# Operand sums among the last row stages, shorter column steps, stored low parts and two more banks for the chains of a fused GLU and spectral kernel

## The chip, the cores and the metric

The kernel runs on one core of one Trainium2 chip. The metric is device time in microseconds (us) for one execution; where several executions are shown, their median counts. Five engines work side by side and meet at semaphores: TensorE (PE, with its weight loads PEld), VectorE (DVE), ScalarE (ACT), GpSimd (POOL) and SyncE (SP). POOL and SP mainly issue DMAs here, each in the order of its own queue, and each waits in that queue until the data of a transfer is ready.

## The reference

For 2048 tokens of 576 features the reference mixes two branches with a gate per token:

```python
g = sigmoid((x * gate_w).sum(-1, keepdims=True))
a = irfft2(rfft2(x) * (w_r + 1j * w_i), s=(S, D))           # S = 2048, D = 576
b = (gelu(x @ w_gate) * (x @ w_up)) @ w_down                # 576 -> 4608 -> 576
return g * a + (1 - g) * b
```

Everything is float32.

## The kernel before, in words

**The dense branch.** It is all on PE. Each float32 operand is split into a high and a low part of a format that PE takes in one pass, and a product is three matmuls (high by high, low by high, high by low). The 4608 hidden features are 36 tiles of 128, taken in 18 blocks of two; the tokens are two halves of 1024, and each half is two pieces `tb` of 512. `chain` (L717) makes one hidden tile of the gate or the up projection for one piece: 14 matmuls of 512 columns into one PSUM bank `pgu`, of which there are two. `hidden` (L757) calls two chains, then GELU on ACT (L767), the product with the second bank on DVE (L771), a high copy on ACT and a low part on DVE (L775). `down` (L805) multiplies such tiles with the down weights, 24 matmuls of 288 columns for a pair of token tiles, into the two buffers of `pdn`, which ACT scales and moves out (L814); POOL then adds the result in DRAM (`yd`, L802). Weights come by SP into `raws`, ACT copies their high part into `gu` or `dn` (L213), and DVE makes the low part (L708).

**The products.** In the second token half, from block `FIRST` on, `products` (L1001) replaces the eight chains of a block by a scheme of seven block products with 14 matmuls each, which needs the sums and differences of quarters of the input, `s1` to `s4`. `operands` (L882) makes these on DVE and ACT in three pieces, from inputs that `load_xs` (L878) brings into `xraw`.

**The spectral branch.** It runs on DVE and ACT beside the chains, in a generator: `forward_rows` (a transform along the features, L481) for each token half, `first_tiles` (L401, a radix-4 step over the tiles with its twiddle factors), `columns` (L234), `last_tiles` (L414) and `inverse_rows` (L532) for each half. Its results are scaled by the gate and added in DRAM. The column stage goes through 16 blocks, pipelined over 18 steps of `STEP` gaps each. In one step `g` counts gaps: a forward product on PE at `g` 0 (`product`, L269, six matmuls of 290 columns into the tile `pf2` of two banks), its real part copied out at 1, the filter at 2, the weights at 5, the end of the filter at 6; the inverse product of the block before at 4, copied out at 5. Two rows of each block have to change places: `corner` (L249) sends them out to `cns` and back by four small DMAs, the first pair two steps ahead at `g` 0, the second at `g` 3; the high copy that reads the block is at `g` 1 of the next step. A second generator, `beside`, fills what is left with radix-4 steps over the tiles.

**The order.** The order of all work is written out by the Python code. `gap()` (L635) is called twice in every chain and after every `down`; there it takes steps of the generator. Each yielded cost is charged against a credit that PE work earns, so the vector work is spread evenly along PE's. Each engine executes its own list in order. What is late in an engine's list holds back everything behind it.

Of the kernel before, what the change touches and what calls it, by code (L numbers as in the profile page):

```python
# [30 lines left out]
STEP = 7  # L31
FIRST = 5
# [71 lines left out]
def _twiddles(eng, act, unit, real, imag, places, tmps, sgn, cost):  # L104

    todo = list(places)

    def scaled(i):
        if i < len(todo):
            at, n = todo[i]  # L110
            s = 1.0 if n == 4 else sgn * math.sin(math.pi * n / 8)
            act.activation(tmps[i % len(tmps)][0], unit(*at), AF.Copy, scale=s)

    yield None
    for i in range(2):
        scaled(i)
    yield None
    for i, (at, n) in enumerate(todo):
        scaled(i + 2)
# [6 lines left out]
        eng.scalar_tensor_tensor(xr, xr, c, ti, op0=ALU.mult, op1=ALU.subtract)  # L126
        yield cost
        eng.scalar_tensor_tensor(xi, xi, c, tr, op0=ALU.mult, op1=ALU.add)
        yield cost
# [28 lines left out]
def _build(nc, tc, a):  # L158
    with ExitStack() as ctx:
# [3 lines left out]
        spec = ExitStack()  # L163
        psf = spec.enter_context(tc.tile_pool(name="psf", bufs=1, space=bass.MemoryType.PSUM))
# [39 lines left out]
        def ps_f2():  # L204
            return psf.tile([P, 2, 512], F32, name="pf2", tag="pf2", bufs=1)

        ps7 = []

        def ps_one():
            return ps7[0].tile([P, TB], F32, name="pone", tag="pone", bufs=2)  # L210
# [19 lines left out]
        def columns():  # L230
# [38 lines left out]
            def product(d, kb, h, l):  # L269
                v = ps_f2()  # L270
# [22 lines left out]
            def beside():  # L293

                more = gates()
                for d in range(1, 4):
                    yield from four(d, TAKEN, sp, -1)
                    made[0] = d
# [4 lines left out]
                yield from more  # L303

            for s in range(2):
                for kb in range(2):
                    load_cc(s, kb)
            yield from four(0, TAKEN, sp, -1)
# [13 lines left out]
            for kb in range(18):  # L322
# [18 lines left out]
                for g in range(STEP):  # L341
# [29 lines left out]
                    elif g == 5:  # L371
                        if was:
                            copy(two(Z[kb - 1]), w[:, :, :NK])
# [3 lines left out]
                    elif g == 6:  # L377
# [9 lines left out]
            gone[0] = 20 * STEP  # L387
            for c in side.pop():
                yield c
# [11 lines left out]
        def first_tiles(h):  # L401

            sp = tmp[:, 0:2 * SW].rearrange("p (e k) -> p e k", e=2)
            tmps = [tmp[:, SW * i:SW * (i + 1)] for i in range(4)]
            tmps = [(x, x[:, 0:NK], x[:, NK:]) for x in tmps]
# [3 lines left out]
            places = [((k, TAKEN[o]), o * k) for k in range(1, 4) for o in range(1, 4) if TAKEN[o] // 2 == h]  # L409
            yield from _twiddles(vec, act, lambda d, e: T[:, d, e], lambda d, e: T[:, d, e, re],  # L410
                                 lambda d, e: T[:, d, e, im], places, tmps, -1, 0.5)
            yield None

        def last_tiles():  # L414
# [3 lines left out]
            tmps = [rows[:, SW * i:SW * (i + 1)] for i in range(4, 8)]  # L418
            tmps = [(x, x[:, 0:NK], x[:, NK:]) for x in tmps]
            places = [((k, LEFT[o]), o * k) for k in range(1, 4) for o in range(1, 4)]  # L420
            yield from _twiddles(vec, act, lambda d, e: T[:, d, e], lambda d, e: T[:, d, e, re],
                                 lambda d, e: T[:, d, e, im], places, tmps, 1, 0.5)
# [109 lines left out]
        def inverse_rows(h):  # L532
            rows = rows_tile()
            T, R = spread(h, rows)
            pl.memset(rows.rearrange("p (c k) -> p c k", c=2)[:, :, 8 * KF:], 0.0)
            yield from moved(lambda t, c: (R[:, c, t, 0:KF], T[:, t, c, 0:KF]))
# [5 lines left out]
            if h == 1:  # L542
                load_xs(0)
# [18 lines left out]
            ))  # L562
            R = rows.rearrange("p (k t) -> p t k", t=8)
            yield None
            if h == 1:
                c = cns.rearrange("p q k -> p (q k)")
                spare_rows = (c[:, 0:D], c[:, D:2 * D], misc[:, SW:SW + D])
                todo_t = list(range(8))
                work = operands()
                n = 0  # L570
                while todo_t or not ops.get("done"):
                    if n % 5 == 0 and todo_t:
                        t = min(todo_t, key=lambda t: abs(count[0] - added[8 + t] - 11))
                        o = spare_rows[len(todo_t) % 3]
                        todo_t.remove(t)
                        act.activation(o, R[:, t, 0:D], AF.Copy, scale=gs[:, 8 + t:9 + t])
                        at(2, lambda t=t, o=o: pl.dma_start(yd[8 + t], o, accum_op=ALU.add))
                    n += 1
# [41 lines left out]
        side = []  # L620
        credit = [0.0]
# [83 lines left out]

        def lower(key, g, r, cost):
            def run():
                vec.tensor_tensor(g[:, 1], r, f(g[:, 0]), ALU.subtract)  # L708
                credit[0] -= cost

# [11 lines left out]

        def chain(j, s, tb):
            due(("gu", j))
            ps, w = ps_gu(), gu[j % 3]
# [13 lines left out]
        def first_chains():  # L739

            v = ps_f2()
            ps = [v[:, c] for c in range(2)]
# [139 lines left out]
        def operands():  # L882

            sx = pool.tile([P, 16 * SW], F32R, name="sx", tag="til")
            s4 = pool.tile([P, 2 * UNIT], F32R, name="s4", tag="tmp")
            parts = [sx[:, 2048 * i:2048 * (i + 1)].rearrange("p (l t k) -> p l t k", l=2, t=2) for i in range(3)]
            parts.append(s4[:, 0:2048].rearrange("p (l t k) -> p l t k", l=2, t=2))
            tails = [sx[:, 6144 + TB * i:6144 + TB * (i + 1)] for i in range(6)] + [s4[:, 2048:2560]]
            for i in range(4):
                ops["s1 s2 s3 s4".split()[i]] = (parts[i][:, 0], parts[i][:, 1], tails[i])  # L890
            ops["a11"] = (xhi[0][:, 0:2], xlo[0][:, 0:2], tails[4])
            ops["a12"] = (xhi[0][:, 2:4], xlo[0][:, 2:4], tails[5])
            ops["a22"] = (xhi[1][:, 2:4], xlo[1][:, 2:4], tails[6])
            m = misc[:, 0:TB]
            for i in range(3):
                if i:
                    load_xs(i)
                    for _ in range(6):
                        yield None
                a11, a12, a21, a22 = (xraw[:, q] for q in range(4))  # L900
                if i == 2:
                    yield from tails_of([(ops[n][2], x) for n, x in (("a11", a11), ("a12", a12), ("a22", a22))])
                for o, x, z, op in ((m, a21, a22, ALU.add), (a21, a11, a21, ALU.subtract),
                                    (a11, m, a11, ALU.subtract), (a12, a12, a11, ALU.subtract)):
                    vec.tensor_tensor(o, x, z, op)
                    yield 0.72
                sums = (("s1", m), ("s2", a11), ("s3", a21), ("s4", a12))
# [3 lines left out]
                else:  # L911
# [4 lines left out]
                    for n, x in sums:  # L916
                        vec.tensor_tensor(ops[n][1][:, i], x, f(ops[n][0][:, i]), ALU.subtract)
                        yield 0.72
            ops["done"] = True
# [183 lines left out]
        for s in range(2):  # L1103
            copy(g1[:, 0, :, s], w1[:, :, s])
            vec.tensor_tensor(g1[:, 1, :, s], w1[:, :, s], f(g1[:, 0, :, s]), ALU.subtract)  # L1105
        aux += [lambda: None] * 2
# [4 lines left out]
        aux += [lambda: None] * 6  # L1111
        one, fin = gate_part(0, rows0)
        for t in range(8):
            aux.append(lambda t=t: one(t))
        aux.append(lambda: [fin(), gens.append(spectral(rows0))])
        for u in range(8):
            aux.append(lambda u=u: release(u))
# [8 lines left out]
        def reload_x(tb):  # L1126
            for k in range(KT):
                i = KT * tb + k
                aux.append(lambda i=i, k=k: [prep_x(tb, k, xraw[:, i % 4]), load_x(i + 4)])

# [55 lines left out]

        for _, _, key in prev[3]:
            due(key)
        spec.close()
        ps7.append(ctx.enter_context(tc.tile_pool(name="ps7", bufs=1, space=bass.MemoryType.PSUM)))  # L1190
# [66 lines left out]
```

## Time and profile before

| | |
|---|---|
| Median of three executions | 1381.41 us (1381.4, 1381.41, 1383.15) |
| The profiled execution's own time | 1383.23 us |
| Its span, first to last instruction | 1381.5 us |
| ScalarE (ACT) busy | 698.4 us, 51% |
| GpSimd (POOL) busy | 266.6 us, 19% |
| Read from and written to HBM | 110.69 MB, 92.01 MB |

The span is 1.7 us shorter than the profiled execution's own time; the rest lies around the instructions. A busy time is the sum of an engine's records. The records of PE overlap, because matmuls are pipelined, so the pace of PE is read from the starts of its matmuls in the timeline and not from their durations. The list of waits gives, for each pair of lines, the total, the number and the longest of the waits that one ended for the other.

### The profile page before, as it was taken

The numbers are of one execution on the slowest core, as the hardware profiler recorded it, in microseconds if no ns is written. First come the engines' busy times: TensorE is split into PE (matmuls) and PEld (weight loads), VectorE is DVE, ScalarE is ACT, GpSimd is POOL, SyncE is SP. The second block draws the span as 40 slices with busy tenths as digits, with TensorE's granted clock in tenths as the row PEclk, the third lists the DMA queues.
The fourth block names the chain that finished last, engine by engine and source line by source line (L and its number), as shares of the span: only waits on it lengthen the run. The fifth ranks groups of instructions, "written<-read, shape, count | busy, mean of one in ns | idle before, by whom it ended". The sixth has DMA issues, their size and how long they took to land.

```text
span 1381.5 us, 20055 instructions
## 1 busy us (share of the span) xinstructions
PE 1368.6 (99%) x7504; PEld 1208.8 (88%) x7504; DVE 1118.0 (81%) x1635; ACT 698.4 (51%) x1072; POOL 266.6 (19%) x326
## 2 busy tenths in 40 slices
PE   8999999999999999999999999999999999999998
PEld 7888888888898888888888888888888888888887
DVE  6989998989868767499898999567777777777776
ACT  5543454344565565444456343865555555555552
POOL 0022111222222221212123011421112222221111
PEclk9999999999999999999999999999999999999999
DMA  8366766668999998655776665966666666666676
GB/s 304 117 116 117 175 116 105 117 114 190 218 238 246 247 217 203 126 109 94 150 151 131 177 125 92 232 135 131 125 131 131 131 128 131 129 129 127 130 154 172
DMA packets 97329, 211.17 MB, mean 153 GB/s; under 512 B 11856, under 2 KB 22096, under 8 KB 96848
## 3 DMA queue, kind: packets, MB, share of 16 engines
q0 software_dynamic: 45248, 92.56, 44.1%
q1 hardware_dynamic: 51984, 117.34, 27.4%
q8 instruction: 59, 0.97, 0.3%
q14 instruction: 38, 0.31, 0.1%
HBM read 110.69 MB, written 92.01 MB: 147 GB/s over the span
## 4 chain that ended last, share of the span: by engine, by line
PE 96%; ACT 2%; DMA 1%; issue 0%; DVE 0%; SPq 0%; DVEq 0%; ACTq 0%
PE pdn L789 33%; PE pgu L728 12%; PE pgu L730 12%; PE pgu L729 12%; PE pgu L971 3%; PE pgu L973 3%; PE pgu L972 3%; PE pgu L734 3%; PE pgu L735 3%; PE pone L971 3%; PE pone L973 3%; PE pone L972 3%; PE pf L274 2%; PE pgu L974 2%; PE pone L974 1%
## 5 line engine op out<-in xcount | busy, mean ns | idle before, releaser
L802 POOL DMA_DIRECT2D yd<-stg x264 | 229.8, 871 | 1024.5 <-ACT stg L814 995.8
L814 ACT ACTIVATE stg<-pdn,omg 128x576 f32<-128x576 f32 x272 | 201.9, 743 | 410.0 <-PE pdn L789 319.8
L789 PEld LDWEIGHTS pdn<-dn,hb 128*128 128x128 f32 x2808 | 388.7, 188 | 12.5 <-ACT stg L814 1.0
L789 PE MATMUL pdn<-dn,hb 128*128 128x288 f32 x2808 | 397.0, 295 | 1.0 <-ACT stg L814 0.8
L728 PE MATMUL pgu<-xhi,gu 128*128 128x512 f32 x728 | 285.6, 392 | 3.7 <-ACT gl L767 3.7
L729 PE MATMUL pgu<-xhi,gu 128*128 128x512 f32 x728 | 284.4, 391 | 0.4 <-DVE gu L1105 0.4
L730 PE MATMUL pgu<-xlo,gu 128*128 128x512 f32 x728 | 284.6, 391 | 0.0
L728 PEld LDWEIGHTS pgu<-xhi,gu 128*128 128x128 f32 x728 | 137.1, 188 | 30.6 <-ACT gl L767 5.5
L730 PEld LDWEIGHTS pgu<-xlo,gu 128*128 128x128 f32 x728 | 137.0, 188 | 29.9
L729 PEld LDWEIGHTS pgu<-xhi,gu 128*128 128x128 f32 x728 | 137.0, 188 | 25.3 <-DVE gu L1105 0.7
L767 ACT ACTIVATE gl<-pgu 128x512 f32<-128x512 f32 x91 | 54.5, 598 | 135.6 <-PE pgu L735 131.4
L213 ACT ACTIVATE gu<-raws 128x1280 fp32r<-128x1280 f32 (+3 forms) x86 | 88.8, 1033 | 40.0 <-PE pgu L734 31.1
L771 DVE TENSOR_TENSOR gl<-gl,pgu 128x512 f32<-128x512 f32 x91 | 62.2, 683 | 39.9 <-PE pgu L735 38.4
L775 DVE TENSOR_TENSOR hb<-gl,hb 128x512 fp32r<-128x512 f32 x92 | 63.2, 687 | 37.5 <-ACT hb L213 37.5
L789 PEld LDWEIGHTS pdn<-dn,gu 128*128 128x128 f32 x624 | 85.6, 188 | 1.9
L789 PE MATMUL pdn<-dn,gu 128*128 128x288 f32 x624 | 86.8, 295 | 0.0
L734 PE MATMUL pgu<-xtl,gu 128*128 128x512 f32 x182 | 70.8, 389 | 0.0
L735 PE MATMUL pgu<-xtl,gu 128*128 128x512 f32 x182 | 70.8, 389 | 0.0
L708 DVE TENSOR_TENSOR gu<-raws,gu 128x1280 fp32r<-128x1280 f32 x44 | 65.3, 1484 | 1.3 <-ACT gu L213 1.3
L989 DVE TENSOR_TENSOR xraw<-xraw 128x512 f32<-128x512 f32 x52 | 36.0, 693 | 28.8 <-ACT xraw L997 28.3
L213 ACT ACTIVATE hb<-gl 128x512 fp32r<-128x512 f32 x92 | 57.3, 623 | 0.0
L1006 DVE TENSOR_TENSOR gl<-gl,pgu 128x512 f32<-128x512 f32 x52 | 35.6, 684 | 25.7 <-PE pgu L974 25.7
(214 smaller groups left out, 2211.9 us busy)
## 6 DMA issues: line engine op xcount, KB each, us to landing
yd<-stg POOLq DMA_DIRECT2D x264, 288.0 KB, 5.0
raws<-wgu SPq DMA_DIRECT2D x44, 640.0 KB, 4.7
raws<-wd SPq DMA_DIRECT2D x72, 288.0 KB, 2.9
colm<-col POOLq DMA_DIRECT2D x32, 256.0 KB, 6.0
raws<-ws SPq DMA_DIRECT2D x21, 384.0 KB, 5.2
quads<-ws SPq DMA_DIRECT2D x20, 384.0 KB, 4.4
tmp<-wf SPq DMA_DIRECT2D x16, 290.0 KB, 5.8
cns<-til SPq DMA_DIRECT2D x64, 72.5 KB, 4.9
```

The lines of the kernel that those rows point to most:

```text
L213: act.activation(o, i, AF.Copy)
L728: pe.matmul(ps, w[:, 0, k, c], xhi[tb][:, k], start=k == 0, stop=False)
L729: pe.matmul(ps, w[:, 1, k, c], xhi[tb][:, k], start=False, stop=False)
L730: pe.matmul(ps, w[:, 0, k, c], xlo[tb][:, k], start=False, stop=False)
L734: pe.matmul(ps, w[:, 0, 4, c], xtl[tb], start=False, stop=False)
L735: pe.matmul(ps, w[:, 1, 4, c], xtl[tb], start=False, stop=True)
L789: pe.matmul(ps[half], h[:, l, c], d[:, q, half * HD:(half + 1) * HD], start=part == 0 and n == 0, stop=part == 1 and n == 2)
L802: pl.dma_start(yd[u], o, accum_op=ALU.add)
L814: put(u, lambda o: act.activation(o.rearrange("p (c k) -> p c k", c=2), v[:, :, 0:HD], AF.Copy, scale=omg[:, u:u + 1]), i == 0)
L971: pe.matmul(ps, hi[:, c], xh[:, t], start=t == 0, stop=False)
L972: pe.matmul(ps, lo[:, c], xh[:, t], start=False, stop=False)
L973: pe.matmul(ps, hi[:, c], xl[:, t], start=False, stop=False)
```

## The change

- **`FIRST` goes from 5 to 4.** One block more of the second token half is made by `products`, so the operands must be ready one block sooner.
- **Operand sums among row stages.** `operands` runs from `woven` inside the last `inverse_rows`: after every second step of the row stages it may take one step, at most until it yields None in the same gap. The fourth sum is put aside (`fourth`) and finished by `last_operand` afterwards. The eight result rows of that half go through five places instead of three.
- **Tile twiddles.** The twiddles of `first_tiles`, and those for two of the three digits in `last_tiles`, go into `beside`, with two temporaries instead of four, so that ACT scales one ahead and not two.
- **`STEP` goes from 7 to 6.** The inverse product's copy moves from `g` 5 to `g` 4, straight behind the product, the filter's weights from 5 to 4, the filter's end from 6 to 5.
- **Low parts.** For the first eight tiles of the hidden features (`2 * FIRST`) the low parts of the weights are written to DRAM in the first token half, and in the second half an SP transfer brings them back in place of DVE's subtraction.
- **Banks.** `pf2` and the two banks that the products used (`pone`) become one tile `px` for the whole program. Outside the column stage (`wide`) the chains of even tiles write to `px`, those of odd tiles to `pgu`, so a bank comes around after four chains.

```diff
-STEP = 7
-FIRST = 5
+STEP = 6
+FIRST = 4
...
+        px = psum.tile([P, 2, 512], F32, name="px", tag="px", bufs=1)
...
+                tmps = [flat[:, SW * i:SW * (i + 1)] for i in (1, 2)]
                 for d in range(1, 4):
+                    yield from tile_twiddles(d, TAKEN, -1, tmps)
                     yield from four(d, TAKEN, sp, -1)
...
+                for k in (1, 2):
+                    yield from tile_twiddles(k, LEFT, 1, tmps)
...
                         if was:
                             w = product(1, kb - 1, yh, yl)
-                    elif g == 5:
-                        if was:
                             copy(two(Z[kb - 1]), w[:, :, :NK])
                         if on:
                             vec.tensor_tensor(z, z, two(w0), ALU.mult)
                             vec.tensor_tensor(vs, vs, w1, ALU.mult)
-                    elif g == 6:
+                    elif g == 5:
...
+        def woven(main, other):
+
+            n, free = 0, 0
+            for v in main:
+                yield v
+                n += 1
+                if n % 2 == 0 and reloaded[0] and count[0] > free:
+                    w = next(other, 0.0)
+                    if w is None:
+                        free = count[0]
+                    else:
+                        yield w
+            yield from other
...
+            yield from woven(inverse_stages(rows), operands() if h else iter(()))
...
         def lower(key, g, r, cost):
+            j, i = key[1], key[0] == "dn"
+            if NT <= j < NT + 2 * FIRST:
+                nc.sync.dma_start(f(g[:, 1]), lows[j - NT][i])
+                return
+
             def run():
                 vec.tensor_tensor(g[:, 1], r, f(g[:, 0]), ALU.subtract)
                 credit[0] -= cost
+                if j < 2 * FIRST:
+                    at(2, lambda: nc.sync.dma_start(lows[j][i], f(g[:, 1])))
...
         def chain(j, s, tb):
             due(("gu", j))
-            ps, w = ps_gu(), gu[j % 3]
+            ps, w = px[:, s] if wide[0] and j % 2 == 0 else ps_gu(), gu[j % 3]
```

Three places show how the lists move. The first is PE's list outside the column stage, where one hidden tile ends and the chain of the next, an even tile, begins. Before, that chain writes to `pgu` like every other:

```order
L734 MATMUL pgu<-xtl_71,gu_73 128x512
L735 MATMUL pgu<-xtl_71,gu_73 128x512
L789 MATMUL pdn<-dn_78,hb_82 128x288 x6
L789 MATMUL pdn<-dn_79,hb_83 128x288 x6
L789 MATMUL pdn<-dn_78,hb_82 128x288 x6
L789 MATMUL pdn<-dn_79,hb_83 128x288 x6
L728 MATMUL pgu<-xhi_66,gu_74 128x512
```

Now it writes to `px`:

```order
L764 MATMUL pgu<-xtl_68,gu_70 128x512
L765 MATMUL pgu<-xtl_68,gu_70 128x512
L818 MATMUL pdn<-dn_75,hb_79 128x288 x6
L818 MATMUL pdn<-dn_76,hb_80 128x288 x6
L818 MATMUL pdn<-dn_75,hb_79 128x288 x6
L818 MATMUL pdn<-dn_76,hb_80 128x288 x6
L758 MATMUL px<-xhi_63,gu_71 128x512
```

The matmuls of an ordinary chain are the same; only the bank alternates by the tile.

The second is ACT's list in the last ordinary blocks. Here `stg` is the result of a `down`, `gl` the GELU, `hb` the high part of a hidden tile, `sx` and `s` the operands, and L576 or L593 a result row of the spectral branch. Before, near the end of the operands, a GELU stands behind copies of tails:

```order
L213 ACTIVATE hb_83<-gl_85 128x512
L213 ACTIVATE sx<-xraw 32x512 x4
L213 ACTIVATE s_7337<-xraw 32x512 x2
L767 ACTIVATE gl_84<-pgu 128x512
L213 ACTIVATE sx<-misc 128x512
```

Now the copies of tails stand further ahead in the program, behind a GELU and behind the evacuation of a `down`:

```order
L796 ACTIVATE gl_81<-px 128x512
L211 ACTIVATE sx<-xraw 32x512 x6
L211 ACTIVATE gu_71<-raws 128x1280
L211 ACTIVATE sx<-xraw 128x512 x3
L796 ACTIVATE gl_82<-pgu 128x512
L843 ACTIVATE stg_84<-pdn,omg 128x576
L211 ACTIVATE hb_79<-gl_81 128x512
L843 ACTIVATE stg_85<-pdn,omg 128x576
L211 ACTIVATE sx<-xraw 32x512 x6
L593 ACTIVATE xraw<-rows,gs 128x576
```

The GELU `gl_81` reads a bank of `px`, which only the chain after the next three needs again, where the one before read one of two banks.

The third is ACT's list in the column stage, where `til<-pf` or `til<-px` is a column product that is copied out and `colm<-til` the high copy for the next product. Before:

```order
L213 ACTIVATE hb_81<-gl_85 128x512
L213 ACTIVATE til<-pf_3321 128x580
L767 ACTIVATE gl_84<-pgu 128x512
L213 ACTIVATE colm<-tmp 128x580
L213 ACTIVATE til<-pf_3363 128x290
L213 ACTIVATE colm<-til 128x580
```

Now, with `xraw<-til` as the scaling for a tile twiddle, which was not there before:

```order
L211 ACTIVATE hb_80<-gl_82 128x512
L211 ACTIVATE til<-px 128x290
L211 ACTIVATE colm<-til 128x580
L113 ACTIVATE xraw<-til 128x580 x2
L796 ACTIVATE gl_81<-pgu 128x512
L336 ACTIVATE tmp<-til 64x580
```

Fifteen such scalings come into this stage, nine for the forward and six for the inverse direction.

More of the change, by code (lines that the diff above doesn't have):

```diff
@@ L114, in _twiddles @@
     yield None
-    for i in range(2):
+    for i in range(ahead):
         scaled(i)
@@ L620, in _build @@
         side = []
+        reloaded = [False]
         credit = [0.0]
@@ L891, in operands @@
[L891 to L894, printed above, removed]
-            for i in range(3):
[L896 to L900, printed above, removed]
+            tails = [sx[:, 6144 + TB * i:6144 + TB * (i + 1)] for i in range(6)]
```

127 lines of the change are left out of this document (76 added, 51 removed).

## The prediction

> **What bounds the kernel now.** I read the page first, then the waits of PE, then PE's starts in the timeline.
>
> ```profile
> PE 1368.6 (99%) x7504; PEld 1208.8 (88%) x7504; DVE 1118.0 (81%) x1635; ACT 698.4 (51%) x1072; POOL 266.6 (19%) x326
> PEclk9999999999999999999999999999999999999999
> ```
>
> PE works all the time at the full clock. So only two things can shorten this program: fewer matmuls, or the little that PE loses between them. All other engines have room on the whole; what matters is whether they have it in the stage in which PE needs them. The waits of PE, whole list but for the load of the first inputs:
>
> ```profile
> PE pgu L728 <- ACT gl L767: 3.7, 3, 2.2
> PE pgu L1090 <- DVE gate L1086: 1.5, 1, 1.5
> ...
> PE pdn L789 <- ACT stg L814: 0.8, 1, 0.8
> ```
>
> In all, PE waited 3.7 us for a PSUM bank that ACT's GELU had not released and 0.8 us for a buffer of `pdn` that ACT had not moved out. The 1.5 us are the start. The longest wait, in the timeline of PE, with the pace before and behind it:
>
> ```profile
> 895.14 0.39 PE L728 MATMUL pgu<-xhi,gu 128*128 128x512 f32 x1
> 895.37 0.39 PE L729 MATMUL pgu<-xhi,gu 128*128 128x512 f32 x1
> 895.60 0.39 PE L730 MATMUL pgu<-xlo,gu 128*128 128x512 f32 x1
> ...
> 898.63 0.50 PE L728 MATMUL pgu<-xhi,gu 128*128 128x512 f32 x1 [2.19 <-ACT gl L767]
> ...
> 899.75 0.63 PE L728 MATMUL pgu<-xhi,gu 128*128 128x512 f32 x1
> 900.17 0.63 PE L729 MATMUL pgu<-xhi,gu 128*128 128x512 f32 x1
> ...
> 902.62 0.39 PE L729 MATMUL pgu<-xhi,gu 128*128 128x512 f32 x1
> ```
>
> A matmul of 512 columns starts 0.23 us after the one before it. After the wait of 2.19 us they start 0.42 us apart, until 902.62. From 898.63 to 902.62 there are ten matmuls; at 0.23 us they take 2.3 us, and they took 4.0. The wait cost 2.2 us and 1.7 us more.
>
> **Part by part: fewer matmuls.** A block of ordinary chains has 8 chains of 14 matmuls, 112; the block that replaces it has 7 products by 2 projections by 7 matmuls, 98. The down matmuls are the same. So 14 matmuls of 0.23 us go: **-3.2 us**, certain as long as PE stays full, since PE is the path that sets the end.
>
> **The banks.** Why ACT was late at 898 stands in its own timeline:
>
> ```profile
> 894.11 2.55 ACT L213 ACTIVATE sx<-xraw 32x512 fp32r<-32x512 f32 x4
> 896.69 1.27 ACT L213 ACTIVATE s<-xraw 32x512 fp32r<-32x512 f32 x2
> 897.98 0.60 ACT L767 ACTIVATE gl<-pgu 128x512 f32<-128x512 f32 x1
> ```
>
> Six copies of tails stand in ACT's list ahead of the GELU, 3.8 us. The same kind of wait, of 1.3 us, lies at the tile twiddles of `last_tiles`, where scalings hold ACT:
>
> ```profile
> PE pgu L728 <- ACT gl L767: 1.3, 1, 1.3
> ```
>
> Both are outside the column stage, where the chains now go round four banks. A bank was needed again after one other chain, some 3.2 us (14 by 0.23); now after three others and the downs between them. Six copies can't hold that up. So the 3.7 us and the slow pace of 1.7 us behind the longest go: **-5.4 us**. The 0.8 us at `pdn` has two buffers as before, but its cause, operands, tails and result rows in one stretch just ahead of the products, is thinned out; I count it as gone, **-0.8 us**, with a new wait there possible (below). In the rows the slow pace follows a wait of 2.2 us. The Trainium skill, "TensorE: Matmul & The Clock Gate", section "What's actually happening", has the clock go to half only after an idle window of about 3.4 us; by that rule the wait would have cost only itself, and the sum below would be -4.4 us instead of -6.1. The trace does not agree, with half the pace behind 2.19 us.
>
> **The column stage.** It is in the windows of the stages, here the columns, the last row stages, the operands, and the densest part of the columns (PE, PEld, DVE, ACT and POOL busy, granted clock, DMA share, GB/s):
>
> ```profile
> 341.00:560.00 219.00, 218.96 (x1241) 195.75 (x1240) 159.73 (x265) 126.59 (x197) 51.41 (x69) 1.00 0.94 222
> 580.00:858.00 278.00, 276.68 (x1505) 243.88 (x1504) 256.62 (x329) 131.00 (x204) 52.03 (x60) 1.00 0.66 131
> 858.00:918.00 60.00, 57.05 (x306) 49.80 (x305) 30.25 (x45) 45.61 (x65) 17.57 (x20) 0.97 0.77 165
> 420.00:460.00 40.00, 39.96 (x230) 35.68 (x229) 31.86 (x56) 23.36 (x38) 10.38 (x14) 1.00 1.00 242
> ```
>
> Eighteen steps of 7 gaps in 219 us are 1.74 us a gap and 12.2 us a step; with 6 gaps the stage lasts about 31 us less. This is not a gain by itself, since PE's chains only move to another place. It pays for the block that goes: the operands must be ready earlier by a block of chains, 112 by 0.23 us, and of four runs of downs like
>
> ```profile
> 30.02 3.18 PE pdn L789 x24
> ```
>
> so by 25.8 and 12.7, some 38 us. DVE has room for it: 159.7 us busy of 219. Into it come the twiddles, 13 of the 15 with two DVE instructions of
>
> ```profile
> 584.44 0.45 DVE L128 SCALAR_TENSOR_TENSOR til<-til,rows 128x290 f32<-128x290 f32 x1
> ```
>
> that is 26 by 0.45, 11.7 us. Out go the chains' instructions of 31 us, some 8 us by an estimate (in the 19 us that two hidden tiles take on PE, half of those 38, a GELU product and a low part twice at 0.69 and the weights' low parts below, about 5 us). So 163 us in 188: 87% where it was 73%. That fits, with less cover. How thin the cover is:
>
> ```profile
> DVE til L92 <- DMA til<-cns: 4.1, 2, 2.2
> ACT colm L213 <- DMA til<-cns: 1.7, 1, 1.7
> PEld pf L274 <- DVE colm L267: 0.3, 1, 0.3
> ```
>
> In this stage PE waited once for an operand of a column product, 0.3 us, and ACT and DVE three times for the two rows that come back by DMA. Two covers shrink by a gap of 1.74 us: the return of those rows to the high copy that reads them, and the low part of the next forward product. Two don't: filter to inverse product, and the inverse product's copy to the next forward product, two gaps each as before. Below nothing it can't cost, since PE has nothing left to win there but 0.3 us. Its other end is every one of 16 steps late by the whole gap, 28 us. I take **+3 us**, near the lower end, because the nearest row is one wait of 0.3 us with the DMA engines already full.
>
> **Low parts and operand sums.** In the second half DVE is spared 8 low parts of each kind,
>
> ```profile
> L708 DVE TENSOR_TENSOR gu<-raws,gu 128x1280 fp32r<-128x1280 f32 x44 | 65.3, 1484 | 1.3 <-ACT gu L213 1.3
> L708 DVE TENSOR_TENSOR dn<-raws,dn 128x576 fp32r<-128x576 f32 x72 | 54.1, 752 | 0.0
> 895.75 0.69 DVE L905 TENSOR_TENSOR xraw<-xraw 128x512 f32<-128x512 f32 x1
> ```
>
> 8 by 2.24, 17.9 us. The operand sums and low parts that move in among the row stages are 24 by 0.69, 16.6 us. In a stage that is 92% full on DVE (256.6 of 278) the two cancel, and the row stages keep their pace; a late GELU product there meets four banks. The loads take
>
> ```profile
> raws<-wgu SPq DMA_DIRECT2D x44, 640.0 KB, 4.7
> raws<-wd SPq DMA_DIRECT2D x72, 288.0 KB, 2.9
> ```
>
> as the transfers of the same size do, 4.7 and 2.9 us, and are issued as soon as the weight buffer is free, half a block (some 19 us) or more before its first chain. They stand in SP's queue, behind a wait for PE's last chain with that buffer, with the next weights and the loads of `xraw` behind them; the buffers are two tiles ahead, so I cost them at nothing, and at 5 us once, a landing, if that cover is gone. The stores follow their low part by two gaps, in the first four blocks, far ahead of the column stage. In the operands' stretch the column of ACT is what is full, 45.6 of 60. Its copies now come earlier, and where they come thickest a `pdn` buffer could be late: 0 to 2 us, and I take **+0.3 us**, as DVE's wait for them is gone from there and ACT's list there holds no transfer but through the five places.
>
> **The sum.** -3.2 - 5.4 - 0.8 + 3 + 0.3 = -6.1 us. The profiled execution took 1383.2 us, its span was 1381.5, so that one would come to 1377.1. It was at the upper end of the three; from their median, 1381.4, I predict **1375.3 us**.
>
> **The rivals.** *The rows that change places set the column step.* This one ends slower. Its row is the DMA share, 0.94 in the stage and 1.00 in its densest part, and the queues there:
>
> ```profile
> q0 software_dynamic: 9935, 19.43, 48.6%
> q1 hardware_dynamic: 17328, 28.95, 44.7%
> ...
> til<-cns SPq DMA_DIRECT2D x58, 72.5 KB, 4.4
> ...
> cns<-til SPq DMA_DIRECT2D x56, 72.5 KB, 5.1
> ```
>
> The rows leave at the head of one step and are read at the second gap of the next: 7 gaps, 12.2 us, where there were 8, 13.9. Out and back take 9.5 us by the median, and SP's queue also holds weight loads that wait. By the share the stage's own transfers are (0.94 - 0.66) by 219, 61 us; in 188 us they make 0.66 + 0.33, 0.99. In the densest part a step's own DMA time is 0.34 by 12.2, 4.1 us, and with 0.66 by 10.4 for the rest a step of 10.4 us needs 11.0. If that lets eight of 16 steps come late by a gap, it is 14 us: 1381.4 - 9.4 + 14 = **1386.0 us**. It decides once SP's own delay passes 2.7 us (12.2 less 9.5) and ACT's delay behind it passes what two banks allow, for here the chains have two. Against it: at 0.94 to 1.00 the landings are 4.4 and 5.1 us, and PE waited 0.3. The Trainium skill, "Trainium Kernel Development and Optimization", section "Key Constraints", says that DMAs of SP, ACT and POOL share the same 16 engines; it speaks for this rival, and the two queues' shares, which add up to the stage's, agree.
>
> *DVE is late in the column stage.* The twiddles have two temporaries, so DVE waits for a scaling that stands in ACT's list behind work that waits for PE. The nearest row is
>
> ```profile
> L126 DVE SCALAR_TENSOR_TENSOR til<-til,rows 128x290 f32<-128x290 f32 x8 | 3.6, 455 | 4.7 <-ACT rows L112 4.7
> ```
>
> 4.7 us in 8 with four temporaries. If half of the 16 inverse products come 1 us late, it is 8 us: **1380.0 us**, no change. Against it: 25 us of DVE are free there.
>
> *Only the matmuls count.* ACT's lump moves from the GELU to `pdn`, which still has two buffers, and PE waits there as long as before: 1381.4 - 3.2 = **1378.2 us**. For it: the 0.8 us at `pdn` fell in the same lump.
>
> That the change doesn't do what it says is no rival: the order shows 7490 matmuls where there were 7504.
>
> **How the numbers follow.** The forecast, with the column stage at 0 to 6 us and the rest as above (1371.5 to 1378.5): 0.70. The rows that change places: 0.13. DVE late: 0.10. Only the matmuls: 0.07. A measurement of this kernel tells 0.2%, 2.8 us, from no change. Faster (below 1378.6): 0.70, with 0.03 of DVE late and 0.05 of only the matmuls, 0.78. Slower (over 1384.2): 0.09 of the first rival. Same: 0.13. The range goes from 1371.0, the sum with no new wait (1381.4 - 9.4 = 1372.0) and another microsecond of small ones, to 1381.5, with all but the first rival in it.
>
> **What would show it.** Right: PE's wait for `pgu` or `px` behind the GELU is gone; no matmuls start 0.42 us apart after the start-up; the column stage lasts some 190 us at 0.98 or more of the DMAs; PE's waits for a column product's operand add up to about 3 us; the products begin some 40 us earlier. Wrong: waits on `til<-cns` of 10 us or more in ACT's or DVE's list; a row of PE behind ACT's `stg` of several us; a PE that is as full as before in an unchanged time.

## The result, and the profile after

| | before | after |
|---|---|---|
| Median | 1381.97 us (five executions, 1381.4 to 1383.25) | 1501.05 us (five, 1499.56 to 1505.04) |
| Span of the profiled execution | 1381.5 us | 1500.6 us |

The changed kernel is slower by 119 us: 1.0864 times the time before, with a 95% interval of 1.0847 to 1.0882. The prediction was 1375.3 us, the upper end of its range 1381.5.

The page of the changed kernel, to be laid beside PE's row of the kernel before:

```profile
PE 1396.9 (93%) x7490; PEld 1207.0 (80%) x7490; DVE 1122.5 (75%) x1649; ACT 701.7 (47%) x1079; POOL 266.3 (18%) x326
...
PEclk9999999999999999999999999999999999999999
```

PE is down from 99% to 93% and no other engine is fuller: DVE went from 81% to 75%, ACT from 51% to 47%. So no other engine became the bound, and the granted clock stayed at nine tenths or more in every slice. PE waits more often. Its waits, the two longest rows and the one of the column products:

```profile
PE px L1013 <- DVE xraw L1048: 48.3, 42, 1.7
PE px L758 <- ACT gl L796: 37.3, 32, 4.7
PE px L272 <- DVE colm L265: 4.0, 2, 2.3
```

The wait for GELU that the change was to remove stood at 3.7 us; it is 37.3 us now, in 32 waits of 1.2 us on the average. And a wait that was not in PE's list before, for DVE's additions in `products` (L1048), takes 48.3 us. Both are for the new tile `px`. In the groups these are the lines:

```profile
L758 PE MATMUL px<-xhi,gu 128*128 128x512 f32 x256 | 106.3, 415 | 37.3 <-ACT gl L796 37.3
L758 PE MATMUL pgu<-xhi,gu 128*128 128x512 f32 x440 | 172.8, 393 | 2.6 <-ACT gl L796 2.6
L1013 PE MATMUL px<-xhi,gu 128*128 128x512 f32 x112 | 47.2, 421 | 27.3 <-DVE xraw L1048 27.3
L1013 PE MATMUL px<-sx,gu 128*128 128x512 f32 x56 | 23.6, 421 | 21.0 <-DVE xraw L1048 21.0
```

L758 stands four times in a chain, so 256 matmuls are 64 chains, 32 pairs: one wait for each pair. The 110 chains in `pgu` waited once. L1013 stands twice in a block product, so 168 matmuls are 84 products in `px`, 42 pairs of a gate and an up product: again one wait for each pair. What happens at such a pair shows in the timeline of PE and ACT:

```profile
583.99 0.39 PE L765 MATMUL px<-xtl,gu 128*128 128x512 f32 x1
584.68 0.58 ACT L796 ACTIVATE gl<-px 128x512 f32<-128x512 f32 x1
585.32 0.50 PE L758 MATMUL px<-xhi,gu 128*128 128x512 f32 x1 [0.94 <-ACT gl L796]
```

At 583.99 the last matmul of the chain into the first bank of `px` starts. ACT reads that bank from 584.68 on. The next chain goes to the *second* bank, which nothing reads at that time, and yet it starts only when ACT is done. In the products it is the same, with DVE as the reader:

```profile
954.19 0.69 DVE L1048 TENSOR_TENSOR xraw<-gl,px 128x512 f32<-128x512 f32 x1
954.93 0.50 PE L1013 MATMUL px<-sx,gu 128*128 128x512 f32 x1 [1.68 <-DVE xraw L1048]
955.27 0.39 PE L1014 MATMUL px<-sx,gu 128*128 128x512 f32 x1
955.50 0.40 PE L1015 MATMUL px<-sx,gu 128*128 128x512 f32 x1
```

The cost is spread over the whole program. The row stages of the last spectral part and a stretch of the products, in the windows (PE, PEld, DVE, ACT and POOL busy, granted clock, DMA share, GB/s):

```profile
575.00:820.00 245.00, 231.19 (x1219) 199.03 (x1218) 214.11 (x271) 109.38 (x171) 45.53 (x54) 0.99 0.67 146
990.00:1360.00 370.00, 337.00 (x1816) 288.79 (x1815) 249.83 (x396) 166.47 (x252) 64.99 (x75) 1.00 0.62 119
```

PE issued 1219 matmuls in 245 us and 1816 in 370 us; below stand the same windows without the wait.

### The profile page after: what moved, and what is told of

Read it like the earlier page. It is cut to its first block, busy times and chain, and to the rows that moved or that the text cites. A ratio compares the mean times of both kernels' runs of the same rounds, so it can differ in the third digit from the quotient of the medians.

```text
span 1500.6 us, 20072 instructions
## 1 busy us (share of the span) xinstructions
PE 1396.9 (93%) x7490; PEld 1207.0 (80%) x7490; DVE 1122.5 (75%) x1649; ACT 701.7 (47%) x1079; POOL 266.3 (18%) x326
## 3 DMA queue, kind: packets, MB, share of 16 engines
q0 software_dynamic: 45248, 92.56, 40.7%
## 5 line engine op out<-in xcount | busy, mean ns | idle before, releaser
L818 PE MATMUL pdn<-dn,hb 128*128 128x288 f32 x2760 | 389.8, 295 | 0.2 <-DVE raws L872 0.2
L758 PE MATMUL pgu<-xhi,gu 128*128 128x512 f32 x440 | 172.8, 393 | 2.6 <-ACT gl L796 2.6
L759 PE MATMUL pgu<-xhi,gu 128*128 128x512 f32 x440 | 172.4, 392 | 0.4 <-DMA gu<-lo 0.4
L760 PE MATMUL pgu<-xlo,gu 128*128 128x512 f32 x440 | 172.1, 391 | 0.0
L758 PE MATMUL px<-xhi,gu 128*128 128x512 f32 x256 | 106.3, 415 | 37.3 <-ACT gl L796 37.3
L759 PE MATMUL px<-xhi,gu 128*128 128x512 f32 x256 | 103.2, 403 | 0.0
L760 PE MATMUL px<-xlo,gu 128*128 128x512 f32 x256 | 102.8, 402 | 0.0
L760 PEld LDWEIGHTS pgu<-xlo,gu 128*128 128x128 f32 x440 | 83.0, 189 | 18.1
L758 PEld LDWEIGHTS pgu<-xhi,gu 128*128 128x128 f32 x440 | 83.0, 189 | 17.8 <-ACT gl L796 3.0
L758 PEld LDWEIGHTS px<-xhi,gu 128*128 128x128 f32 x256 | 49.5, 193 | 59.4 <-ACT gl L796 50.8
L759 PEld LDWEIGHTS pgu<-xhi,gu 128*128 128x128 f32 x440 | 83.0, 189 | 15.7 <-DMA gu<-lo 0.8
L796 ACT ACTIVATE gl<-pgu 128x512 f32<-128x512 f32 x55 | 32.8, 597 | 125.5 <-PE pgu L765 111.8
L1048 DVE TENSOR_TENSOR xraw<-gl,px 128x512 f32<-128x512 f32 x56 | 38.5, 688 | 60.8 <-PE px L1016 58.3
L1013 PE MATMUL px<-xhi,gu 128*128 128x512 f32 x112 | 47.2, 421 | 27.3 <-DVE xraw L1048 27.3
```

Of the source, the lines that this page charges most:

```text
L758: pe.matmul(ps, w[:, 0, k, c], xhi[tb][:, k], start=k == 0, stop=False)
L759: pe.matmul(ps, w[:, 1, k, c], xhi[tb][:, k], start=False, stop=False)
L760: pe.matmul(ps, w[:, 0, k, c], xlo[tb][:, k], start=False, stop=False)
L818: pe.matmul(ps[half], h[:, l, c], d[:, q, half * HD:(half + 1) * HD], start=part == 0 and n == 0, stop=part == 1 and n == 2)
L1013: pe.matmul(ps, hi[:, c], xh[:, t], start=t == 0, stop=False)
L1048: vec.tensor_tensor(o, x, v, ALU.add)
```

## The experiments

**Theory A: a tile is the unit of the wait.** `px` is one tile of two banks. What writes to one of its banks is held until the readers of the other are done, since the framework that builds the program orders work by tile. Two tiles of one bank each would take the wait away. **Theory B**, the rival: the second bank's wait is ACT's or DVE's delay, or the column stage's, so a split of the tile changes little. By a rule of the Trainium skill, "PSUM — Partial Sum Buffer", section "PSUM bank collisions raise a hardware error", PSUM is to be guarded by bank; a matmul into one bank beside a reader of another needs no guard. The trace of `two_tiles` (below) agrees: there a GELU reads one bank for 0.60 us from 581.35 on, and matmuls into the other start at 581.54 and 581.77. In the changed kernel the program itself guards it. Its list for PE, with what an instruction waits for:

```text
L765 MATMUL px<-xtl_67,gu_72 128x512
L758 MATMUL px<-xhi_63,gu_72 128x512 [waits Activation_49]
```

So the wait is written into the instruction that opens the second bank.

**1. `two_tiles`**: `px` as two tiles of one bank.

```diff
-        px = psum.tile([P, 2, 512], F32, name="px", tag="px", bufs=1)
+        px = [psum.tile([P, TB], F32, name=f"px{i}", tag=f"px{i}", bufs=1) for i in range(2)]
...
-            ps, w = px[:, s] if wide[0] and j % 2 == 0 else ps_gu(), gu[j % 3]
+            ps, w = px[s] if wide[0] and j % 2 == 0 else ps_gu(), gu[j % 3]
...
-                            copy(two(Z[kb - 1]), w[:, :, :NK])
+                            for c in range(2):
+                                copy(two(Z[kb - 1])[:, c], w[c][:, :NK])
```

> The changed kernel with px as two tiles of one bank each in place of one tile of two banks (the column product is copied out by two instructions). Theory A, the two banks are one tile and PE's matmuls for one bank wait for the GELU or the sum that reads the other: the 37 us of waits for px in the chains and the 48 us in the products go, with the slower pace behind them; in the stages PE lost 61 us in the products and about 45 us in the ordinary chains over the kernel before, so about 1393 us (1385 to 1402). Theory B, the late work of DVE and ACT and the DMAs' load make GELUs and sums late and PE would wait on any bank: over 1470 us.

Measured: 1391.4 us (four executions, 1388.28 to 1393.31), 1.0059 times the kernel before, interval 1.0042 to 1.0075. Splitting the tile returns 109.7 of the 119 us. In the program's list the matmul that opens the second bank no longer waits for ACT but for DVE, the earlier reader of its own bank:

```text
L766 MATMUL px_113<-xtl_67,gu_72 128x512
L759 MATMUL px_114<-xhi_63,gu_72 128x512 [waits DVE_49]
```

The same two windows:

```profile
575.00:820.00 245.00, 241.44 (x1304) 212.38 (x1303) 226.41 (x293) 115.75 (x180) 44.43 (x52) 0.99 0.72 167
990.00:1360.00 370.00, 370.00 (x2054) 328.48 (x2054) 280.70 (x443) 189.10 (x286) 73.45 (x85) 1.00 0.70 130
```

1304 matmuls in place of 1219, and 2054 in place of 1816; in the products PE doesn't wait at all.

**2. `pgu_chains`**: the one tile kept for the column stage and the products, all chains on `pgu`.

```diff
-            ps, w = px[:, s] if wide[0] and j % 2 == 0 else ps_gu(), gu[j % 3]
+            ps, w = ps_gu(), gu[j % 3]
```

> The changed kernel with all chains on the two banks of pgu; px is used by the column products and the block products alone. Theory A: the products keep their 61 us, the chains win some 40 to 45: about 1458 us (1450 to 1468). Theory B: no difference beyond 10 us, about 1495.

Measured: 1460.37 us, one execution. Its waits of PE:

```profile
PE px L1013 <- DVE xraw L1048: 48.3, 42, 1.7
PE pgu L758 <- ACT gl L796: 6.2, 3, 4.1
```

The wait in the products is there to the tenth of a microsecond. Of the chains' waits for a GELU 6.2 us are left, now for `pgu`.

**3. `old_banks`**: the edit of `pgu_chains`, and the banks of the column stage and the products as before, two pools one after the other and `pone` two tiles; the rest of the change kept.

```diff
-        px = psum.tile([P, 2, 512], F32, name="px", tag="px", bufs=1)
+        psf = spec.enter_context(tc.tile_pool(name="psf", bufs=1, space=bass.MemoryType.PSUM))
...
-            return px[:, ones[0] % 2]
+            return ps7[0].tile([P, TB], F32, name="pone", tag="pone", bufs=2)
```

> The changed kernel with the banks of before: chains on pgu, pf2 until the products begin, then two tiles pone. Theory A: as with two tiles, without what four banks save: about 1397 us (1388 to 1406). Theory B: over 1470 us.

Measured: 1394.66 us (four executions, 1392.21 to 1397.22), 1.009 times, interval 1.0071 to 1.0109. With `pgu_chains` this prices the two places: `px` in the products costs 1460.4 - 1394.7 = 65.7 us, in the chains 1501.05 - 1460.4 = 40.7 us. Both prices rest on the one execution of `pgu_chains`.

**4. `before_px`**: the kernel before with the change's banks alone, as one tile; steps, twiddles, low parts and operands as before.

> The kernel before with the banks of the change alone: px as one tile for column products, block products and the chains of even tiles. Theory A: 1382 and 13/14 of 61 us in the products and about 45 us in the chains, so about 1483 us (1470 to 1495). Theory B: 1382 us within 5.

Measured: 1499.15 us, one execution, 4 us over the upper end of what was expected. Its waits of PE:

```profile
PE px L729 <- ACT gl L767: 46.2, 33, 5.4
PE px L971 <- DVE xraw L1006: 44.9, 39, 1.7
```

The bank edit alone costs the kernel before 117.5 us (1499.15 against 1381.67), nearly the 119 us of the whole change. The prices of the parts don't add up, for the rest of the change, with the old banks, costs 13 us more (`old_banks`). Theory A holds, theory B is out.

**What is left: 10 us in `two_tiles`.** With the tile mended the forecast's sum should hold, but the time is 1391.4, not 1375.3. The longest of its waits of PE, and three of ACT and DVE that belong to the column stage:

```profile
PE px L272 <- DVE colm L265: 4.0, 2, 2.3
PE pgu L760 <- DMA gu<-lo: 3.6, 1, 3.6
PE pgu L759 <- ACT gl L797: 2.6, 1, 2.6
...
DVE til L377 <- ACT tmp L211: 14.0, 10, 2.4
ACT colm L211 <- DMA til<-cns: 13.2, 6, 5.9
DVE til L127 <- ACT xraw L113: 9.7, 6, 3.6
```

Three causes offer themselves: **C**, the two rows that change places, at the tighter step (`til<-cns`); **D**, the tile twiddles, with DVE behind ACT's scaling (L127 behind L113); and once a load of a low part (`gu<-lo`). The next runs keep the two tiles and take one thing away each.

**5. `two_step7`**: seven gaps a step again (`STEP = 7`, copy and weights at `g` 5, the filter's end at 6), twiddles kept.

> Two tiles for px, and the column stage with the 7 gaps of before (copy of the inverse product at 5, weights at 5, end of the filter at 6); the rest of the change stays, tile twiddles in the stage and FIRST = 4 too. With two tiles and 6 gaps PE lost some 16 us in the column stage. Theory C, the rows that change places are too late by DMA: a gap more gives them 1.7 us more, the waits on til<-cns go below 6 us, the stage loses 0 to 4 us, 1378 us (1375 to 1382). Theory D, the tile twiddles with two temporaries make DVE late: they stay, so most of the 16 us stays, 1387 us or more.

Measured: 1383.27 us (ten executions, 1380.42 to 1384.0), 1.0007 times, interval 0.9997 to 1.0017. By its time it lies between the two, above C's range and below D's. Its waits say more. In the column stage PE waits 1.7 us, where in `two_tiles` it waits 9.3 (the 4.0 and the 2.6 above, and 2.1 and 0.6 more), and ACT has no wait for `til<-cns` left. So with seven gaps the twiddles cost little in their stage. The time goes at the start of the products, where a sum of weights on DVE (L996) waits for a result row that is still being read out of `cns`, and PE for the low part behind it (L1003):

```profile
DVE cns L996 <- DMA yd<-cns: 3.9, 1, 3.9
...
PE px L1017 <- DVE gu L1003: 3.4, 1, 3.4
PE px L272 <- DVE colm L265: 1.7, 1, 1.7
PE pdn L821 <- ACT stg L846: 1.6, 1, 1.6
```

What was won in the columns was given back in part there.

**6. `two_notw`**: six gaps kept, the twiddles back in `first_tiles` and `last_tiles`, with four temporaries.

```diff
-                    yield from tile_twiddles(d, TAKEN, -1, tmps)
...
-                for k in (1, 2):
-                    yield from tile_twiddles(k, LEFT, 1, tmps)
...
-            yield from tile_twiddles(3, LEFT, 1, [rows[:, SW * i:SW * (i + 1)] for i in range(4, 8)])
+            for k in (1, 2, 3):
+                yield from tile_twiddles(k, LEFT, 1, [rows[:, SW * i:SW * (i + 1)] for i in range(4, 8)])
```

> Two tiles for px, 6 gaps, and the tile twiddles back in first_tiles and last_tiles (four temporaries); DVE has 12 us less to do in the column stage. Theory C: the waits on til<-cns stay at 8 us or more and the stage loses 10 us or more, 1389 us (1385 to 1393). Theory D: the stage loses 0 to 4 us, 1378 us.

Measured: 1372.11 us, one execution; D, and better than D's own number. The same program was run again in five executions:

> The same program as two_notw, timed in five rounds: two tiles for px, 6 gaps, FIRST = 4, operand sums among the row stages, low parts from DRAM, all tile twiddles in first_tiles and last_tiles. From its one look 1372 us (1370.5 to 1374), faster than the kernel before by 0.6 to 0.8%.

Measured: **1372.0 us** (1371.45 to 1373.71), 0.9933 times the kernel before, interval 0.992 to 0.9945. It is the fastest version of the study and beats both kernels. Its page, the longest of its waits of PE, and ACT's wait for the rows in the column stage:

```profile
PE 1363.4 (99%) x7490; PEld 1207.2 (88%) x7490; DVE 1118.5 (82%) x1649; ACT 703.8 (51%) x1095; POOL 265.2 (19%) x326
```

```profile
PE pgu L1135 <- DVE gate L1131: 1.5, 1, 1.5
...
ACT colm L211 <- DMA til<-cns: 6.7, 4, 2.5
```

Of PE's waits only the start is left, and 0.2 us at the end. ACT still waits 6.7 us for the rows, and PE does not feel it. Its column stage, and the same stretch of `two_tiles`, where the stage runs from 332 to 540 us:

```profile
343.00:533.00 190.00, 190.00 (x1081) 170.22 (x1080) 151.72 (x254) 119.39 (x200) 45.24 (x62) 1.00 0.99 240
```

```profile
343.00:533.00 190.00, 184.44 (x1030) 163.84 (x1029) 149.40 (x255) 114.83 (x194) 43.82 (x60) 0.98 0.95 230
```

With the twiddles out, the DMA engines are fuller (0.99) and PE has no gap. With the twiddles in, all that runs there is less busy, DVE too (149.4 of 190, 79%): engines wait for each other in turn. How this comes about is seen in `two_tiles` at PE's longest wait for a column product's operand:

```profile
534.87 0.69 ACT L211 ACTIVATE colm<-tmp 128x580 fp32r<-128x580 f32 x1 [3.07 <-DVE tmp L342]
...
537.95 0.46 DVE L127 SCALAR_TENSOR_TENSOR til<-til,xraw 128x290 f32<-128x290 f32 x1 [0.95 <-ACT xraw L113]
...
538.69 0.76 DVE L265 TENSOR_TENSOR colm<-tmp,colm 128x580 fp32r<-128x580 f32 x1
...
539.51 0.80 PE L272 MATMUL px<-colm 128*128 128x290 f32 x4 [2.30 <-DVE colm L265]
```

The high copy starts at 534.87. The low part that goes with it (L265) starts only at 538.69, because twiddles stand ahead of it in DVE's list, and DVE waits 0.80 us (up to 536.17) and 0.95 us for their scalings on ACT. No run keeps the twiddles in the stage with four temporaries, so their place and the two temporaries are not told apart.

**7. `two_edge`**: the rows that change places are sent ahead of a load in SP's queue, so they come earlier; twiddles kept.

```diff
+                            corner(kb + 2, 0, False)
                             load_ww(kb + 1)
-                            corner(kb + 2, 0, False)
```

> Two tiles for px, 6 gaps, and at the head of a column step the edge rows are sent out before the filter's weights are loaded, in place of behind them; nothing else changes. Theory C: out and back become shorter by what two loads of 290 KB take in the queue, 1 to 3 us; the waits on til<-cns fall from 13 us to less than half, the stage loses 5 to 12 us in place of 16, 1385 us (1379 to 1388). Theory D: no difference beyond 2 us, 1391 us.

Measured: 1387.32 us (five executions, 1386.44 to 1387.79), 1.0042 times, interval 1.0027 to 1.0056. The time is in C's range and 4.1 us below `two_tiles`; the two intervals overlap, so the waits have to decide. ACT's waits for the rows fell from 13.2 to 1.6 us. Of PE's waits these two stayed:

```profile
PE px L272 <- DVE colm L265: 4.0, 2, 2.3
PE pgu L760 <- DMA gu<-lo: 3.9, 1, 3.9
```

The wait of 2.6 us for a GELU is gone, and one for the copy of a column product fell from 2.1 to 0.7 us. In `two_tiles` that GELU stood in ACT's list behind the rows:

```profile
402.06 0.69 ACT L211 ACTIVATE colm<-til 128x580 fp32r<-128x580 f32 x1 [5.86 <-DMA til<-cns]
402.65 0.58 ACT L797 ACTIVATE gl<-pgu 128x512 f32<-128x512 f32 x1
403.28 0.50 PE L759 MATMUL pgu<-xhi,gu 128*128 128x512 f32 x1 [2.62 <-ACT gl L797]
```

So C carries about 4 us, which D's "no difference beyond 2 us" missed, but only in company with the twiddles: in `two_notw_again` ACT waits 6.7 us for the rows and PE not at all.

**8. `before_step6`**: the kernel before with six gaps and nothing else (copy and weights at `g` 4, the filter's end at 5).

> The kernel before with the column steps of the change alone (6 gaps, the copy and the weights at 4, the end of the filter at 5); banks, twiddles, FIRST = 5 and low parts as before. Theory C: the column stage loses 6 to 14 us here too: 1392 us (1388 to 1397). Theory D: DVE has room without the twiddles, less than 3 us: 1383 us.

Measured: 1384.38 us, one execution. The column stage lasts 189 us, and no wait of PE lies in it. It is 3 us over the kernel before (1381.47). What it loses is elsewhere, from 877 us on, behind a GELU among the operands' copies:

```profile
PE pgu L726 <- ACT gl L765: 5.3, 3, 4.4
```

The shorter step is harmless in itself; it moves the lump at the operands.

**9. `before_two`**: the kernel before with four banks as two tiles of one, nothing else.

> The kernel before with four banks for the chains alone, px as two tiles; FIRST = 5, 7 gaps, twiddles and low parts as before. The prediction's term: the 3.7 us of waits behind the GELU and 1.7 us of slow pace go, 1376 us (1374 to 1378). Rival, ACT's lump only moves the wait to pdn: 1380 to 1382 us.

Measured: 1376.97 us (five executions, 1376.19 to 1377.27), 0.9966 times, interval 0.9953 to 0.998. Against the kernel before, timed beside it at 1381.26, it is 4.3 us less. No wait of PE for GELU is left; the one at `pdn` grew from 0.8 us:

```profile
PE pdn L790 <- ACT stg L815: 1.4, 1, 1.4
```

**10 and 11. `two_fwd` and `two_inv`**: of the twiddles, only the forward ones (nine) or only the inverse ones (six) in the column stage; the others as in `two_notw`.

> two_tiles with the forward tile twiddles in the column stage and the inverse ones back in last_tiles. Theory D, scalings and two temporaries make DVE and ACT late wherever they stand: the waits of PE before 420 us stay, some 9 us, those near 500 to 540 us go: 1382 us (1378 to 1387, up to 5 us of it by the load of a low part at some 735 us). Rival E, only the entry counts: 1389 to 1392 us, as with all of them.

> two_tiles with the inverse tile twiddles in the column stage and the forward ones back in first_tiles. Theory D: the waits of PE near 500 to 540 us stay, some 8 us, those before 420 us go: 1380 us (1376 to 1385). Rival E: 1371 to 1374 us, as with none of them.

Measured: 1381.58 us with the forward ones (ten executions, 1379.63 to 1385.05; 1.0005 times, interval 0.9995 to 1.0014), 1375.16 us with the inverse ones (four, 1373.87 to 1375.81; 0.9953 times, interval 0.9939 to 0.9967). The time of the first is as D says, and E is out. The second lies between D's range and E's, and D's waits near 500 to 540 us are not there: 0.5 us of waits of PE are left in the column stage, with the forward twiddles 4.7, with both 9.3. Against 1372.0 the forward twiddles cost 9.6 us, the inverse ones 3.2 (its interval overlaps that of `two_notw_again`), and both together 19.4. They don't add up. The waits behind the scaling, with the forward ones and then with the inverse ones:

```profile
DVE til L127 <- ACT xraw L113: 8.0, 4, 3.5
```

```profile
DVE til L127 <- ACT xraw L113: 2.9, 2, 2.1
```

Some 5 of the missing 6.6 us lie at the load of the low part. In `two_tiles` PE stands still for it once, from 737 us on, and eight matmuls behind the wait start 0.42 us apart in place of 0.23:

```profile
724.54 0.46 SPq L731 DMA_DIRECT2D gu<-lo  x1
...
737.31 0.39 PE L759 MATMUL pgu<-xhi,gu 128*128 128x512 f32 x1
741.25 0.50 PE L760 MATMUL pgu<-xhi,gu 128*128 128x512 f32 x1 [3.56 <-DMA gu<-lo]
```

It was issued 13 us ahead and took about 16.7 us, among transfers that are as slow there (window 690 to 760, median us from issue to landing at the end of the row):

```profile
yd<-til POOLq DMA_DIRECT2D x8, 288.0 KB, 12.0
gu<-lo SPq DMA_DIRECT2D x3, 640.0 KB, 9.5
```

With the inverse twiddles alone that wait is 0.6 us, with the forward ones or with none it is not in the list. SP had also issued 1.9 MB of loads in the 6.5 us ahead of it; whether these or the additions made it late was not shown. Whether the load falls among them depends on when the stages fall; that the twiddles cause it in any other way was not shown.

## Why the prediction was wrong, step by step

**Fewer matmuls, -3.2 us.** Right: 7490 matmuls, and wherever PE is full they count in full.

**The banks, -5.4 us: the step that failed.** It says "the chains now go round four banks", and that a bank is needed again "after three others and the downs between them". By the memory that is so; by the program it is not, since a tile is reused as a whole. The first chain of an even tile has the distance that the step counted; the second has none, for it writes to a tile that ACT is about to read. That costs 40.7 us in 32 pairs, 1.3 us each. That "a bank comes around after four chains", as the list of changes has it, is wrong for the same reason. The second half of the same edit has no term in the prediction at all: in the products, two tiles of `pone` became two halves of one, at 65.7 us for 42 pairs, 1.6 us each. The diff line `px = psum.tile([P, 2, 512], ...)` and the list of waits in the program show both before any run; the prediction read the order of PE's matmuls and the names of their tiles, but not what each of them waits for. As for the idea, the term was well sized: with two tiles it is -4.3 us, with all of GELU's waits gone.

**`pdn`, -0.8 and +0.3 us.** Right in `two_notw`, where no such wait is left; in `before_two` it grew to 1.4. Too small to matter.

**The column stage, +3 us.** Too small, and wrong in its cause. The step priced the two covers that shrink by a gap. Alone these cost nothing there: `before_step6` and `two_notw` pass the stage in 189 us, as forecast, without a wait of PE. Nor do the twiddles cost much alone: with seven gaps (`two_step7`) PE waits 1.7 us in the stage. Together they cost: PE waits 9.3 us there, and with six gaps the twiddles take 9.6, 3.2 or, together and with what they set off, 19.4 us. The step put 11.7 us of DVE work against the room on DVE and found it to fit at 87%. It does fit; DVE was only 79% busy. What counts is the order, and how much cover the step leaves: a twiddle on DVE waits for a scaling that ACT has in its list behind other work, and the column product's low part stands behind that twiddle on DVE. Room on an engine is no cover for an instruction that waits in its list.

**The rivals.** *DVE is late in the column stage* names this mechanism and was given 0.10. Its 8 us stand against 19.4, of which some 4 come by the rows and some 5 by the load, so about 10 are left for it. *The rows that change places* looked right by the sign that the prediction set for it: the changed kernel has ACT wait 14.1 us for `til<-cns`. The sign was badly chosen, for most of the time is not there: `two_edge` takes the waits away and keeps 15.3 of the 19.4 us, and `two_notw_again` runs the stage at 0.99 of the DMA engines with PE full. *Only the matmuls* is out, for the GELU waits do go with two tiles. None of the rivals held what happened, so the slow end, 1386.0 us, was 115 us short.

**Low parts and operand sums.** That they cancel was right: in `two_notw` PE is full in the row stages and the products begin 40 us earlier, at 868 us against 908 in `before_two`. The loads were costed at "nothing, and at 5 us once, a landing, if that cover is gone": in `two_tiles` it was once, 3.6 us of wait and 1.6 us by the slow pace behind it, near that price.

**The sum without a new wait** was 1372.0 us in the prediction, and is 1372.0 us in `two_notw_again`, the change with two tiles and without the moved twiddles. The term that was measured alone comes near (-4.3 us for the banks in place of -5.4); that the sum agrees to the tenth is luck.

## What to carry to other kernels

In a program that this framework orders, a PSUM buffer's distance of reuse is counted in tiles and not in banks: two banks that shall be filled and read in turn must be two tiles. Before such an edit is priced, read in the program's list what the first instruction into each buffer waits for; a price for buffers that rests on the order alone leaves out the waits. And work that is moved into a stage because an engine has room there has to be followed through the lists of the engines that feed it, above all when the same change makes the steps of that stage shorter; the share of busy time does not tell whether it fits.

## What the runs showed of the hardware

Half the pace after short waits came again. In `two_tiles` a wait of 2.30 us ends at 539.51 (above); soon after, matmuls of 512 columns start 0.42 us apart:

```profile
541.36 0.63 PE L766 MATMUL pgu<-xtl,gu 128*128 128x512 f32 x1
541.79 0.63 PE L759 MATMUL pgu<-xhi,gu 128*128 128x512 f32 x1
```

In the changed kernel's products a wait of 1.68 us leaves the pace at 0.23 us (955.27 and 955.50, above), and the waits there, none over 1.7 us, leave the granted clock at 1.00 (window 990 to 1360). The length alone does not decide. The same wait in the changed kernel is 2.32 us long, and the chain matmuls behind it, from 563.95 to 568.28, start 0.23 us apart:

```profile
563.31 0.80 PE L272 MATMUL px<-colm 128*128 128x290 f32 x4 [2.32 <-DVE colm L265]
```

Behind the start-up, the shortest wait with half the pace behind it in the traces of this case was 2.05 us (`pgu_chains`, ending at 541.96), the longest without it 2.54 us (`before_px`, at 257.36). The Trainium skill, "TensorE: Matmul & The Clock Gate", section "What's actually happening", gives an idle window of about 3.4 us for the fall to half the clock; here 2.05 us sufficed once, so the traces do not agree.

DMA engines at a share of 0.99 for 190 us did not hold PE up (`two_notw_again`); the rows that change places took 4.6 us out and 4.7 us back in `two_notw_again`, by the median, as before the change (5.1 and 4.4). A late load did hold it up, once, where one of 640 KB took about 16.7 us, against a median of 5.9 for the eight such loads of the same run (`two_tiles`).
